# Window attention into a soft mixture of experts on one core: score maxima in nine 128-column products, and three smaller reorderings

## The chip, the core and the metric

The kernel runs on one core of a Trainium2 chip. The metric is the device time of one execution in microseconds (us). Five in-order engines work side by side: TensorE (PE), which multiplies; VectorE (DVE); ScalarE (ACT); GpSimd (POOL), which here also issues most DMAs; and SyncE (SP), which issues the first loads and the stores. They wait for each other through semaphores. TensorE writes to PSUM, eight banks of 2 KB per partition; ACT and DVE read it there.

## What is computed

Shapes: 8 batches, 8 heads, 576 positions, 64 dimensions a head; 4608 rows of 512, 8 experts with 4 slots each, hidden width 1024. Cut to the computation:

```
scores = q @ k.T / 8
mask   = (0 <= i - j < 64)
scores = where(mask, scores, -1e9);  scores -= max over keys
attn   = exp(scores) / (sum + 1e-9)
x      = attn @ v, heads side by side: (4608, 512)

logits = x @ phi                                  # (4608, 32)
d      = exp(logits - max over rows) / sum        # dispatch, per column
slots  = d.T @ x                                  # (32, 512)
out_e  = relu(slots_e @ w1_e) @ w2_e              # 8 experts
c      = exp(logits - max over slots) / sum       # combine, per row
out    = c @ slot_out                             # (4608, 512)
```

## The kernel before, in words

The work is ordered by hand: instructions stand on each engine in the order in which the Python code emits them. The main loop (lines 535 to 624) has 32 iterations `n`, one for each pair of heads (8 batches of 4 pairs), and is a software pipeline. Iteration `n`

- has POOL join pair `n + 1` into transposable order (`join`, L101) and issue coming loads (`load_qk`, `load_v`, `load_w`) and copies of v shifted by half a chunk (`shift_v`);
- turns k and then q of pair `n` through PE (`turn`, L259) into PSUM banks `kb` and `qb`, from which ACT copies them to `kT` (L269) and to `qz` (L266, two copies, one per head, with zeros between so that one product serves both heads);
- finds the largest score of each query of pair `n - 1`: `st_mask` (L274, L275) writes the mask into the PSUM tile `mx`, `st_max` (L291) adds the scores, and DVE reduces them into `m` (L296, `keep_max`);
- turns the maxima of pair `n - 2` through PE (`st_shift`, L300) into the tile `av`, and copies nine rows of them to `rt` (L303, `keep_shift`);
- computes the masked and shifted scores of pair `n - 3`: constants `lh` times `rt` (L320), plus keys times queries (L323), in `sc`, with the ninth chunk apart (`score_last`, L311 and L312), followed by two exponentials on ACT (L328, and L316 for the ninth chunk) into `pt`;
- multiplies `pt` of pair `n - 4` with v (`st_av`, L340) into `av`, and DVE divides by the sums (`st_norm`, L349 and L350) into `x_b`;
- turns `x_b` of pair `n - 5` (L363), and DVE copies it to `xt` (L370).

From `n = 8` on, each batch of rows also has four steps, `fi` = 0 to 3: the logits (L379; copied at L384; maximum at L388 and L389), the dispatch exponentials `dd` (L395) and the turned logits (L403, L408), the slot sums `si` (turned dispatch weights in the same bank as `qb`, copied by ACT to `dT`, L420; sums at L459; accumulation `acc`, L469), and the combine weights (L431, L438, L447). Turns, logits and sums share a ring of two PSUM banks, taken in turn: a product can start when the reader of the bank's last content is done.

A chunk is 64 queries of both heads; its windows lie in 128 keys. In the kernel before, the maxima are found per half chunk: 32 queries of two heads are 64 columns, and their keys lie in a window of 96. So there are 18 products of 64 by 96, ten groups of 96 in the two banks of `mx`, and one reduction over 960 elements; the mask comes from constants of its own (`sel`, `wm`, `wb`), built on POOL and DVE at the start.

After the loop the last pairs and the last two batches are finished, then the experts run: `first`, `turned` and `second` (L796 to L825). The second expert layer of the last `NH` experts, whose weights come last, is done by column halves (`half`, L844): slot outputs for 256 columns, then output rows for these columns (`cps`, L856: product, scaling on ACT or DVE, DMA from SP), then the other 256.

Of the kernel before, what the change touches and what calls it, by code (L numbers as in the profile page):

```python
# [20 lines left out]
def kernel(  # L21
# [114 lines left out]
    for t_, src in reversed(tuple(zip(firsts, (q, k)))):  # L136
# [9 lines left out]
    lh = const.tile([128, 9, 128], FP16, name="lh")  # L146
    nc.vector.memset(lh, 0.0)
    warm = lh[:, 0:4, :].rearrange("p i x -> p (i x)")
    NQ = 4
    qzs = [pqk.tile([128, 2 * S], FP16, name=f"qz{i}") for i in range(NQ)]  # L150
    kTs = [pqk.tile([128, 64 + S], FP16, name=f"kT{i}") for i in range(NQ)]
    sides[0] = (pil.tile([GP, RQ, 2, Dh], FP16, name="qi", tag="qi"),
                pil.tile([GP, RQ, 2, Dh], FP16, name="ki", tag="ki"))
    KR = 74
    nc.scalar.activation(lh[64:KR], ident_h[64:KR, 64:KR - 1].unsqueeze(2).broadcast_to([KR - 64, 9, 128]),
                         AF.Copy, scale=-1.0)
    nc.vector.memset(qzs[0], 0.0)
    nc.vector.memset(kTs[0][:, 0:64], 0.0)
    for t_, src, eng in zip(sides[0], firsts, (nc.scalar.copy, nc.vector.tensor_copy)):
        eng(out=t_, in_=src.rearrange("p (h r d) -> p r h d", h=2, r=RQ))  # L160

    ctr = pmo.tile([128, 2 * S], FP16, name="ctr")
    wb = ctr[0:32, 0:96]
    nc.gpsimd.memset(wb, 0.0)
    nc.gpsimd.affine_select(out=wb, in_=wb, compare_op=ALU.is_gt, fill=NEG,
                            base=0, pattern=[[1, 96]], channel_multiplier=-1)
    nc.gpsimd.affine_select(out=wb, in_=wb, compare_op=ALU.is_ge, fill=NEG,
                            base=64, pattern=[[-1, 96]], channel_multiplier=1)
    mb = ctr[0:64, 96:224]
# [6 lines left out]
    NR = 2  # L176
    sel = const.tile([128, 4, 32], FP16, name="sel")
    wm = const.tile([128, 5, 96], FP16, name="wm")
    for t in (0, 64):
        nc.vector.tensor_copy(out=sel[t:t + 32],  # L180
                              in_=ident_h[t:t + 32, t:t + 32].unsqueeze(1).broadcast_to([32, 4, 32]))
        nc.vector.tensor_copy(out=sel[t + 32:t + 64].rearrange("p (t l) x -> p t (l x)", t=2),
                              in_=ident_h[t + 32:t + 64, t + 32:t + 34].unsqueeze(2).broadcast_to([32, 2, 64]))
        nc.vector.memset(wm[t + 32:t + 64], 0.0)
        nc.vector.tensor_copy(out=wm[t:t + 32], in_=wb.unsqueeze(1).broadcast_to([32, 5, 96]))
    nc.vector.memset(wm[32:33, 0, 0:64], NEG)
    nc.vector.memset(wm[32:34, 0, 0:32], NEG)
    av = pav.tile([128, 2, 512], FP32, name="av", tag="av")
    mx = pmx.tile([128, 2, 512], FP32, name="mx", tag="mx")
    nc.vector.memset(mx[:, 1, 384:480], 0.0)  # L190
    ms = [const.tile([128, 33], FP16, name=f"m{i}") for i in range(2)]
    for t_ in ms:
        nc.vector.memset(t_[:, 10:33], 0.0)
    for t_, z_ in zip(kTs[1:], qzs[1:]):
        nc.vector.memset(t_[:, 0:64], 0.0)
        nc.vector.memset(z_, 0.0)
    nc.vector.memset(av[64:128, :, 260:325], 1.0)
    rts = [const.tile([128, 128], FP16, name=f"rt{i}") for i in range(NR)]
    for rt in rts:
        nc.vector.memset(rt, 0.0)  # L200
    for i in range(3):
        nc.vector.memset(vrs[i][:, :, 64], 1.0)
    for i in range(2):
        nc.vector.memset(vss[i][:, :, 64], 1.0)
        nc.vector.memset(vss[i][0:64, 0, 0:64], 0.0)
    lgs = pf.tile([128, 192], FP32, name="lgs")
    nc.vector.memset(lgs[0:96, 128:192], -3.0e38)
    dd = pf.tile([128, 256], FP16, name="dd")
    nc.vector.memset(dd[:, 192:256], 0.0)
    run = pmo.tile([128, 3], FP32, name="run")  # L210
    stat, nmax = run[:, 0:1], [run[:, 1:2], run[:, 2:3]]
    nc.vector.memset(nmax[1], 1.0e30)
    nc.vector.memset(stat, 0.0)
# [65 lines left out]
    def heads(p, o, w):  # L279
        a = qzs[p % NQ][:, 2 * o:2 * o + 2 * w]  # L280
        return a if w == 32 else a.rearrange("p (t l x) -> p l t x", t=2, l=2)

    def turned_max(p):
        return rts[p % NR][:, :].rearrange("p (t l x) -> p l t x", t=2, l=2)

# [622 lines left out]
```

## Time and profile before

| | |
|---|---|
| three timed runs | 194.35, 195.71, 192.37 us; median 194.35 |
| profiled execution, time | 192.44 us |
| profiled execution, span of the core | 190.7 us |
| busy: PE, PEld, DVE, ACT, POOL | 155.2, 116.2, 139.8, 129.3, 129.8 us |
| granted TensorE clock, mean | 0.889 |
| DMA | 41.14 MB, mean 216 GB/s |

The profile shows one execution. A row of the order of time gives start and length in us, engine, line, operation, result and operands with their shapes; in brackets stands the idle time of the engine just ahead of it and what ended it. Rows of equal instructions in a row are merged (x6). PEld is the loading of weights into TensorE. The ends of products are modelled and overlap, so starts are what to read on PE.

### The profile page before, as it was taken

The page shows a single profiled execution, that of the slowest core. Times are in us where ns is not written, and L with a number is a line of the kernel's source. Part 1 is how long each engine was busy: PE and PEld are TensorE (multiplying, and loading weights), DVE is VectorE, ACT ScalarE, POOL GpSimd, SP SyncE. Part 2 cuts the span into 40 slices and gives each one's busy share as a digit, 9 for nine tenths or more (in the row PEclk, how much of TensorE's full clock was granted, in tenths as well). Part 3 has the DMA queues.
Part 4 walks back from the last instruction along what each step waited for, and adds up shares of the span by engine and source line. Part 5 has one row for each costly group of instructions (what it writes and reads, how often), then busy time and mean ns, then how long its engine had stood idle before and what let it go on. Part 6 is the DMA issues. An engine that isn't in the chain of part 4 may idle for free.

```text
span 190.7 us, 6941 instructions
## 1 busy us (share of the span) xinstructions
PE 155.2 (81%) x2897; PEld 116.2 (61%) x2897; DVE 139.8 (73%) x322; ACT 129.3 (68%) x244; POOL 129.8 (68%) x254
## 2 busy tenths in 40 slices
PE   1858888988898898988989779997888999999400
PEld 0538777867687677776868657676666446564000
DVE  4786688888799979978879987887775754689500
ACT  5672787879778797887977888787664052668400
POOL 8989999976979879888897877965988440000000
PEclk9975699999999999999999999999999699555555
DMA  6999999999999999999999999999999999999996
GB/s 149 148 184 184 201 199 184 173 224 177 184 220 183 183 221 180 185 223 178 182 215 188 188 217 211 198 213 213 217 218 199 198 198 180 249 342 342 399 415 269
DMA packets 64447, 41.14 MB, mean 216 GB/s; under 512 B 38816, under 2 KB 61856, under 8 KB 62880
## 3 DMA queue, kind: packets, MB, share of 16 engines
q0 software_dynamic: 58320, 30.68, 118.1%
q1 hardware_dynamic: 6096, 10.03, 14.6%
q8 instruction: 22, 0.36, 0.7%
q14 instruction: 9, 0.07, 0.1%
HBM read 61.93 MB, written 9.44 MB: 374 GB/s over the span
## 4 chain that ended last, share of the span: by engine, by line
PE 38%; DVE 32%; ACT 11%; issue 10%; POOL 2%; DVEq 0%; ACTq 0%; POOLq 0%
DVE m L296 9%; DVE x_b L350 8%; PE cp L861 7%; PE av L340 6%; ACT qz L266 3%; PE sc L320 3%; PE hh L800 3%; PE sc L323 3%; DVE rt L303 2%; PE ops L823 2%; ACT pt L328 2%; DVE rc L349 2%; PE mx L291 2%; PE qb L259 2%; ACT pt L316 2%
## 5 line engine op out<-in xcount | busy, mean ns | idle before, releaser
L266 ACT ACTIVATE qz<-qb 64x576 f16<-64x576 f16 x64 | 41.2, 643 | 1.8 <-PE qb L259 1.2
L296 DVE TENSOR_REDUCE m<-mx 128x10 f16<-128x960 f32 x32 | 36.8, 1149 | 0.6 <-PE mx L291 0.6
L328 ACT ACTIVATE pt<-sc 128x1024 f16<-128x1024 f32 x29 | 29.6, 1022 | 9.4 <-PE sc L323 8.7
L269 ACT ACTIVATE kT<-kb 128x576 f16<-128x576 f16 x32 | 20.8, 650 | 13.6 <-PE kb L259 13.2
L350 DVE TENSOR_TENSOR x_b<-av,rc 128x640 f16<-128x640 f32 x31 | 25.6, 824 | 1.1
L259 PE MATMUL qb<-ident_h,qi 96*128 96x96 f16 x192 | 14.2, 212 | 8.9 <-DVE acc L469 3.5
L303 DVE CAST rt<-av 9x128 f16<-9x128 f32 x30 | 8.7, 289 | 16.5 <-PE av L300 15.7
L117 POOL DMA_DIRECT2D vr<-in_v_dram x16 | 20.0, 1249 | 0.0
L323 PE MATMUL sc<-qz,kT 128*128 128x128 f16 x232 | 18.6, 223 | 0.7 <-issue 0.7
L320 PE MATMUL sc<-rt,lh 128*128 128x128 f16 x232 | 18.6, 225 | 0.6 <-DVE rt L303 0.6
L291 PE MATMUL mx<-kT,qz 128*64 128x96 f16 x576 | 18.7, 211 | 0.0
L340 PEld LDWEIGHTS <-pt 128*64 128x64 f16 x576 | 12.7, 110 | 9.3 <-ACT pt L316 4.4
L259 PEld LDWEIGHTS <-qi 96*128 96x128 f16 x192 | 11.5, 101 | 10.6 <-issue 9.5
L323 PEld LDWEIGHTS <-kT 128*128 128x128 f16 x256 | 16.5, 100 | 0.9 <-issue 0.9
L108 POOL COPY qi<-qs 96x384 int32<-96x384 int32 x31 | 15.6, 503 | 1.8 <-DMA qs<-in_q_dram 0.9
L320 PEld LDWEIGHTS <-lh 128*128 128x128 f16 x256 | 16.2, 100 | 0.7 <-DVE lh L228 0.4
L108 POOL COPY ki<-ks 96x384 int32<-96x384 int32 x31 | 15.6, 503 | 1.1
L865 ACT ACTIVATE ob<-cp,rcs 128x256 f32<-128x256 f32 (+1 forms) x27 | 13.2, 546 | 3.9 <-PE cp L861 3.6
L291 PEld LDWEIGHTS <-qz 128*64 128x64 f16 x576 | 15.6, 113 | 0.5 <-issue 0.4
L259 PE MATMUL kb<-ident_h,ki 96*128 96x96 f16 x192 | 14.6, 216 | 1.1 <-DVE xt L370 0.6
L340 PE MATMUL av<-vr,pt 128*64 128x65 f16 x279 | 15.4, 197 | 0.0
L340 PE MATMUL av<-vs,pt 128*64 128x65 f16 x279 | 13.7, 198 | 1.8 <-ACT pt L316 1.8
(198 smaller groups left out, 367.8 us busy)
## 6 DMA issues: line engine op xcount, KB each, us to landing
w<-in_moe_w_dram POOLq DMA_DIRECT2D x12, 1024.0 KB, 15.2
vr<-in_v_dram POOLq DMA_DIRECT2D x16, 288.0 KB, 11.8
out_dram<-ob SPq DMA_DIRECT2D x6, 768.0 KB, 7.0
ks<-in_k_dram POOLq DMA_DIRECT2D x15, 288.0 KB, 9.5
qs<-in_q_dram POOLq DMA_DIRECT2D x15, 288.0 KB, 10.3
out_dram<-ob SPq DMA_DIRECT2D x11, 384.0 KB, 4.3
w<-in_moe_w_dram POOLq DMA_DIRECT2D x8, 512.0 KB, 13.8
xt<-in_k_dram SPq DMA_DIRECT2D x1, 288.0 KB, 3.1
```

The costliest lines, as they stand in the source:

```text
L108: nc.gpsimd.tensor_copy(out=d_, in_=s_.rearrange("p h r d -> p r h d"))
L117: nc.gpsimd.dma_start(out=vrs[b % 3][:, c0:c1, 0:64], in_=src[:, c0:c1, :])
L259: nc.tensor.transpose(tp[:, j, :], src[:, j].rearrange("p h d -> p (h d)"), ident_h[0:GP, 0:GP])
L266: nc.scalar.activation(dst[r, hl], src[r], AF.Copy, scale=scale)
L269: nc.scalar.activation(kTs[p % NQ][:, 64:64 + S].rearrange("p (g j) -> p g j", j=RQ), ps[:, 0:RQ * GP].rearrange("p (j g) -> p g j", j=RQ) ...
L291: nc.tensor.matmul(mx[64 * t:64 * t + 64, i // 5, 96 * (i % 5):96 * (i % 5) + 96], heads(p, o, 32), kT[:, o:o + 96], start=False, stop=Tru ...
L296: nc.vector.reduce_max(ms[p % 2][:, 0:10].rearrange("p (h c) -> p h c", h=2), mx[:, :, 0:480].rearrange("p h (c x) -> p h c x", x=96), axi ...
L320: nc.tensor.matmul(sc[:, i // 4 - o, 128 * (i % 4):128 * (i % 4) + 128], lh[:, i, :], turned_max(p), start=(i % 4 == 0), stop=False, skip_ ...
L323: nc.tensor.matmul(sc[:, i // 4 - o, 128 * (i % 4):128 * (i % 4) + 128], kTs[p % NQ][:, 64 * i:64 * i + 128], heads(p, 64 * i, 64), start= ...
L328: nc.scalar.activation(pts[p][:, 0:8, :, :], sc[:, :, :].rearrange("p u (c l x) -> p (u c) l x", l=2, x=64), AF.Exp)
L340: nc.tensor.matmul(av[r0:r0 + 64, hl, 65 * (i // 2):65 * (i // 2) + 65], pt[:, i, hl, :], values(b, h, i), start=True, stop=True, skip_gro ...
L350: nc.vector.tensor_tensor(out=x_b[:, :, 128 * hp:128 * hp + 128].rearrange("p c (l d) -> p l c d", l=2), in0=avv[:, :, :, 0:64], in1=rc[:, ...
```

## The change

1. *Maxima.* `st_max` takes eight products of 128 columns (64 queries of two heads) by 128 keys, and `st_max_last` the ninth, which stands in the free end of a bank of `av`, ahead of `st_av`. The mask comes from constants that the scores use too (`lh`, `rt`) and one small tile `low`; `st_mask` moves from ahead of `st_av` to just ahead of `st_max`, behind the shift. DVE reduces 1024 elements (`keep_max`) and, ahead of that, the ninth chunk's 128 (`keep_max_last`). `qz` is laid out by 64 queries and head. `lh` has nine constant rows instead of ten.
2. *The ninth chunk's scores* go to the end of the bank of `qb` instead of `av`, behind the turn of q. In the iterations with `fi` 0 and 2, ACT copies the shift to `rt` (before: DVE) and makes `qz` and the last exponential only behind it; the logits are copied by ACT instead of DVE.
3. *First constants and joins.* Fewer constants are made ahead of the loop; `vr`, `vs`, `av` and softmax constants follow in iterations 2 and 3. The joins of pairs 3 and 4 and some loads move to the ends of iterations 1 and 2.
4. *The end.* `NH` is 2 instead of 3; the last three output rows of the second quarter are made in whole width after both halves (15 rows by halves instead of 18).

The diff, cut to its core:

```diff
 def st_mask():
-    st = sel.rearrange("p a x -> p (a x)")
-    nc.tensor.matmul(mx[:, 0, 0:480], st[0:64], wm[0:64, 0:5, :], ...)
-    nc.tensor.matmul(mx[:, 1, 0:384]..., st[64:128], wm[64:128, 1:5, :]..., ...)
+    for r, u, keys in ((slice(0, 64), 0, lh[0:64, 0:4, :]),
+                       (slice(64, 128), 1, low[64:128, 1, :].unsqueeze(1).broadcast_to([64, 4, 128]))):
+        nc.tensor.matmul(mx[:, u, :]..., (low[r, 0, :] if u else rts[0][r, :]), keys, ...)
 def st_max(p):
-    for i in range(9):
-        for t in range(2):
-            o = 64 * i + 32 * t
-            nc.tensor.matmul(mx[64 * t:64 * t + 64, i // 5, 96 * (i % 5):96 * (i % 5) + 96],
-                             heads(p, o, 32), kT[:, o:o + 96], ...)
+    for i in range(8):
+        nc.tensor.matmul(mx[:, i // 4, 128 * (i % 4):128 * (i % 4) + 128], queries(p, i),
+                         kTs[p % NQ][:, 64 * i:64 * i + 128], ...)
+def st_max_last(p, to):
+    nc.tensor.matmul(to, rts[0][0:64, :], lh[0:64, 8, :], start=True, ...)
+    nc.tensor.matmul(to, queries(p, 8), kTs[p % NQ][:, 512:640], ...)
+def keep_max_last(p, to):
+    nc.vector.reduce_max(ms[p % 2][:, 8:9], to, axis=AXX)
...
-NH = 3
+NH = 2
...
-    if n + 1 < NP:
+    if n + 1 < NP and n not in (2, 3):
         join(n + 1)
...
         keep_main(n - 3, sc)
-        score_last(n - 3, av[:, 0, 328:456])
-        keep_last(n - 3, av[:, 0, 328:456])
...
     turn(sides[n][0], qb)
-    keep_q(n, qb)
-    if n >= 1:
-        st_mask()
+    if n >= 3:
+        score_last(n - 3, s8)
+    late = fi in (0, 2)
+    if not late:
+        keep_both()
+    m8 = av[:, 0, 328:456]
+    if n >= 1:
+        st_max_last(n - 1, m8)
     if n >= 4:
         st_av(n - 4, av)
...
         st_shift(n - 2, av[64:97, 1, 384:512])
-        keep_shift(n - 2, av[64:97, 1, 384:512])
+        keep_shift(n - 2, av[64:97, 1, 384:512], nc.scalar.copy if fi in (0, 2) else nc.vector.tensor_copy)
+    if late:
+        keep_both()
...
     if n >= 1:
+        keep_max_last(n - 1, m8)
+        st_mask()
         st_max(n - 1)
...
         keep_max(n - 1)
+    if n == 1:
+        join(3)
+        load_v(0, (1,))
+        load_qk(3)
+    elif n == 2:
+        constants(2)
+        join(4)
+        load_qk(4)
+        shift_v(0, 0)
+        load_w(1)
+    elif n == 3:
+        constants(3)
     if fi == 0:
-        keep_logits(lg, nc.vector.tensor_copy)
+        keep_logits(lg, nc.scalar.copy)
...
-        for j0, j1 in ((0, 1), (1, 3), (3, 6), (6, 9)) if h == g == 0 else thirds:
+        for j0, j1 in ((0, 1), (1, 3), (3, 6), (6, 9)) if h == g == 0 else thirds[0:3 - g]:
             cps(g, j0, j1, DH * h, DH * h + DH)
+cps(1, 6, 9)
```

`keep_both` is `keep_q(n, qb)` followed by `keep_last(n - 3, s8)`; `s8` is the last 128 fp32 columns of the bank of `qb`.

160 lines of the change are left out of this document (75 added, 85 removed).

## The prediction

> **What bounds the kernel now.** I read the page first, then busy times in stretches, then one batch of the loop on each engine in order of time, then the queues of the start.
>
> ```profile
> span 190.7 us, 6941 instructions
> ...
> GB/s 149 148 184 184 201 199 184 173 224 177 184 220 183 183 221 180 185 223 178 182 215 188 188 217 211 198 213 213 217 218 199 198 198 180 249 342 342 399 415 269
> ```
>
> ```profile
> 12.00:22.00 10.00, 8.20 (x94) 6.85 (x95) 6.77 (x21) 4.95 (x8) 9.85 (x16) 0.50 1.72 184
> ...
> 65.67:81.53 15.86, 14.48 (x327) 11.83 (x324) 13.65 (x29) 13.40 (x26) 13.76 (x27) 1.00 1.54 195
> ```
>
> The columns of the stretches are length, busy PE, PEld, DVE, ACT, POOL, granted clock, DMA share, GB/s. A batch of four loop iterations takes 15.86 us; no engine fills it, four are within 2.5 us of it. So the batch is set by hand-offs between in-order queues, and the change must be costed along those, not by busy time. I call the four iterations of a batch by what they add: logits, exp, slots, combine (n mod 4 = 0, 1, 2, 3, for n = 8 to 31: six batches). One batch on PE, from the start of its `kb` turn to that of the next batch:
>
> ```profile
> 83.71 0.43 PE L259 MATMUL kb<-ident_h,ki 96*128 96x96 f16 x6
> ...
> 85.35 0.42 PE L259 MATMUL qb<-ident_h,qi 96*128 96x96 f16 x6
> 86.03 0.36 PE L274 MATMUL mx<-wm,sel 64*128 64x480 f16 x1 [0.26 <-DVE m L296]
> ...
> 86.66 0.22 PE L300 MATMUL av<-ident_h,m 128*33 128x128 f16 x1
> ...
> 87.64 0.43 PE L259 MATMUL kb<-ident_h,ki 96*128 96x96 f16 x6
> ...
> 89.95 0.41 PE L259 MATMUL qb<-ident_h,qi 96*128 96x96 f16 x6 [0.59 <-DVE lgs L384]
> 90.30 0.37 PE L274 MATMUL mx<-wm,sel 64*128 64x480 f16 x1
> ...
> 90.89 0.22 PE L300 MATMUL av<-ident_h,m 128*33 128x128 f16 x1
> ...
> 91.42 0.43 PE L259 MATMUL kb<-ident_h,ki 96*128 96x96 f16 x6
> ...
> 94.31 0.22 PE L340 MATMUL av<-vs,pt 128*64 128x65 f16 x1 [0.21 <-ACT pt L316]
> ...
> 94.59 0.22 PE L300 MATMUL av<-ident_h,m 128*33 128x128 f16 x1
> ...
> 95.70 0.43 PE L259 MATMUL kb<-ident_h,ki 96*128 96x96 f16 x6
> ...
> 99.57 0.43 PE L259 MATMUL kb<-ident_h,ki 96*128 96x96 f16 x6
> ```
>
> The iterations take 3.93, 3.78, 4.28 and 3.87 us. PE stands three times: the mask for the maxima (L274) waits for the last reduction to free `mx`, `qb` waits for a bank that DVE still reads (logits, slots), and `av` waits for ACT's last exponential, which reads a bank of `av`. ScalarE and VectorE in the same batch:
>
> ```profile
> 88.11 0.65 ACT L269 ACTIVATE kT<-kb 128x576 f16<-128x576 f16 x1 [0.60 <-PE kb L259]
> 89.06 1.02 ACT L328 ACTIVATE pt<-sc 128x1024 f16<-128x1024 f32 x1 [0.30 <-PE sc L323]
> ...
> 90.58 0.45 ACT L395 ACTIVATE dd<-lgs,run 128x192 f16<-128x192 f32 x1 [0.32 <-DVE run L389]
> ...
> 91.22 1.28 ACT L266 ACTIVATE qz<-qb 64x576 f16<-64x576 f16 x2
> 92.52 0.65 ACT L269 ACTIVATE kT<-kb 128x576 f16<-128x576 f16 x1
> 93.07 1.02 ACT L328 ACTIVATE pt<-sc 128x1024 f16<-128x1024 f32 x1
> 93.97 0.28 ACT L316 ACTIVATE pt<-av 128x128 f16<-128x128 f32 x1
> 94.13 0.31 ACT L420 COPY dT<-qb 128x160 f16<-128x160 f16 x1
> 94.30 1.32 ACT L266 ACTIVATE qz<-qb 64x576 f16<-64x576 f16 x2
> ```
>
> ```profile
> 86.99 0.29 DVE L303 CAST rt<-av 9x128 f16<-9x128 f32 x1 [0.39 <-PE av L300]
> ...
> 87.57 0.82 DVE L350 TENSOR_TENSOR x_b<-av,rc 128x640 f16<-128x640 f32 x1
> 88.31 1.15 DVE L296 TENSOR_REDUCE m<-mx 128x10 f16<-128x960 f32 x1
> 89.38 0.52 DVE L384 COPY lgs<-lg 128x128 f32<-128x128 f32 x2
> 89.93 0.35 DVE L388 TENSOR_REDUCE nb<-lgs 128x1 f32<-128x192 f32 x1
> ...
> 97.31 0.74 DVE L469 SCALAR_TENSOR_TENSOR acc<-acc,al,si 128x512 f32<-128x512 f32 x1
> ```
>
> **The change, part by part.** *The products.* The mask grows from 480 + 256 columns to 512 + 512, and 18 products become 8 of 128 columns, plus two small ones for the ninth chunk. Eight such products have a row, and so has ScalarE's copy of the shift:
>
> ```profile
> 100.00 0.45 PE sc L320 x8
> ```
>
> ```profile
> L303 ACT CAST rt<-kb x2: 256/256/256, 134.7 to 137.3; 9x128 f16<-9x128 f32 x2
> ```
>
> 1024 columns take 0.45 us, so mask and maxima after the shift take 0.05 + 0.45 + 0.45 = 0.95 us, where 90.89 to 91.42 was 0.53 with the mask ahead of it; the ninth chunk is 0.11 us ahead of `av`. On PE it is some +0.25 us per iteration.
>
> *The reduction.* 1024 elements for 960: 64 more at 1.15 us / 960, +0.08 us. The ninth chunk is a reduction of its own, 128 elements: at most the 0.35 us of the 192-element L388, at least the 0.12 us that 128 elements take by L296's rate; I take 0.22. DVE gains 0.3 us per iteration, loses the `rt` copy (0.29) in logits and slots and the logits copies (0.52) to ACT: 13.65 + 4 × 0.3 − 0.58 − 0.52 = 13.75 us a batch, no more than before.
>
> *The order.* Shift no longer stands behind a mask that waits for the reduction, and the last exponential reads `qb`, not `av`, so both PE waits (0.26 and 0.21 us) go. What is late next: in logits and slots the two `qz` copies and the last exponential stand on ACT behind the `rt` copy, which waits for the shift; the next `kb` takes `qb`'s bank and so waits for all three. In exp, the two logits copies stand ahead of `kT` on ACT. In slots, the last score product shares `qb` with the dispatch turn and waits for ACT's copy `dT`. These are waits that the built program has. I add them up, t = 0 at `kb` of logits:
>
> - Logits: `kb` to `qb` 1.64 (83.71, 85.35) less 0.11 for the last score, now later; `qb` 0.35 (89.95, 90.30), last score 0.11, ninth chunk 0.11, `av` 0.28 (94.31, 94.59): the shift starts at 2.38. ACT sees it 0.33 later (86.66, 86.99), 2.71; the copy holds ACT 0.20 of its 0.256; `qz` pair 2.91 to 4.23; exponential at 4.15 for 0.27; next `kb` 4.47. Before 3.93: +0.54.
> - Exp: PE needs 2.38 + 0.95 and reaches the next `kb` at 7.80, unhindered. ACT: logits copies to 4.71, `kT` at 4.47 + 0.47 (87.64, 88.11) = 4.94, main exponential at 4.47 + 1.42 (87.64, 89.06) = 5.89, for 0.90 (93.07, 93.97); `dd` and its two followers 0.64 (90.58, 91.22), `qz` 1.30 (91.22, 92.52), last exponential 0.16 (93.97, 94.13): `kT` of slots at 8.89, 1.1 us after its `kb` instead of 0.47.
> - Slots: `kT` ends 9.54, exponential 9.44 to 10.34, `dT` to 10.65; the last score starts 10.70, shift 10.70 + 0.11 + 0.11 + 0.28 = 11.20, `rt` 11.53, `qz` 11.73 to 13.05, exponential to 13.24, next `kb` 13.29. From `kb` of logits to here it was 95.70 − 83.71 = 11.99: +1.30.
> - Combine: DVE's reciprocal waited in slots for the end of ACT's `rt` (11.79, and 0.05 to hand over, as from 89.38 + 0.52 to 89.95); then 0.29 (0.58 from 86.99 to 87.57, less the copy), 0.74 (87.57, 88.31), 0.22 and 1.15 (88.31, 89.38, + 0.08) put `acc` at 14.24; 0.74 and a hand-over later `qb` starts, 15.03 (PE is there at 14.82); + 0.85 to the shift, + 0.95: 16.83.
>
> 16.83 against 15.86: **+0.97 us a batch, six batches +5.8 us**. Bounds: with ACT's two logits copies at the price of `dT` (0.31 each), `rt` at 0.256 and the exponential unoverlapped it is +1.3 a batch; with the ninth reduction, copies and exponential at their least, and half of the `dT` wait hidden, +0.5. So +3 to +8.
>
> The Trainium skill's page "PSUM — Partial Sum Buffer", in its section on bank collisions, says that no two engines may work in one bank and quadrant at once, reads included. The trace agrees where it can (`av` stood 0.21 us for ACT's read of other columns). That is why the reciprocal waits for `rt`; without the rule it would start 0.3 us earlier, `acc` would be no obstacle, and the sum would be 0.2 us a batch less, 1.2 us in all.
>
> *The start.* DVE's first constants are fewer and end earlier, and pair 3 is joined ahead of two loads. But pair 2's q (11.58) waits for DMA either way, and pair 4's join now stands on POOL ahead of `load_qk(4)`, the first shift of v, a weight load, v and phi.
>
> ```profile
> L117 POOL DMA_DIRECT2D vr<-in_v_dram x16 | 20.0, 1249 | 0.0
> ```
>
> ```profile
> qs<-in_q_dram POOLq DMA_DIRECT2D x1, 288.0 KB, 9.2
> ```
>
> ```profile
> 9.46 0.67 POOL L96 DMA_DIRECT2D qs<-in_q_dram  x1
> ...
> 11.58 0.50 POOL L108 COPY qi<-qs 96x384 int32<-96x384 int32 x1 [0.93 <-DMA qs<-in_q_dram]
> ...
> 21.71 0.52 POOL L108 COPY ki<-ks 96x384 int32<-96x384 int32 x1
> ...
> 24.71 0.43 PE L259 MATMUL kb<-ident_h,ki 96*128 96x96 f16 x6
> ```
>
> The q rows of pair 4 land 9.2 us after their issue at 9.46; issued perhaps 0.6 us earlier, 18.1 to 18.7. Behind that join wait about 5.3 us of POOL work (two k and q issues at 0.67, v issue 1.25, and by like prices the v shift, a weight and phi) until pair 5 is joined at about 24.5 instead of 21.71; its `kb` ran at 24.71 and now needs the join's 0.5 us: 25.0. POOL, busy 9.85 of 10 us there, takes back what DVE gives. I count 0, as 25.0 stands to 24.71; bounds −1.5 (the join waits little) and +1.5 (the delay reaches pair 6).
>
> *Light iterations* (n = 4 to 7) lose the mask wait but stand behind POOL: 0. *After the loop* the ninth chunk of the last pair adds a product and a reduction, +0.3. *The end.* Eight 512-column products in place of eight 256-column ones ahead of the first output cost about 8 × 0.03 us there; the second half starts with eight products and three output rows less before it, and 0.79 MB leaves in whole rows (399 GB/s against 342: −0.3 us). I take −0.3, bounds −1.0 to +0.5. **Sum: +5.8 us.**
>
> The profiled execution took 192.44 us around its span of 190.7; the three runs have a median of 194.35, 1% more. With the profiled one the four average 193.7, and I set the sum on that: 199.5 us.
>
> **The rivals.**
> *ACT's waits are covered; the freed shift decides.* Then the fullest queue sets the batch: DVE 13.75, PE 14.48 + 4 × 0.25 = 15.5 at the modelled busy time, less what that counts double. At 14.7 it is −1.2 a batch, −7 us: 186.5. For it: both PE waits that it removes are in the rows. Against it: ACT had 0.30 to 0.60 us idle ahead of `kT` and `pt` only, and is given 0.2 + 0.4 us more and made to wait twice. It decides if `kb` of exp and combine starts as soon as PE is done with `lg` and `si`.
> *Half of the stalls and an early start.* +0.4 a batch (+2.4), start −1.5: 194.6, no change. For it: my chain adds starts and slots from other iterations, and one hidden hand-over in each of its four steps is worth the difference of 0.5 us a batch. The Trainium skill's "TensorE: Matmul & The Clock Gate" (part 1) has the clock rise to full after about 3.4 us of sustained work; here PE was busy 8.20 of 10 us from 12 to 22 at 0.50, so the trace does not agree closely. If a denser start freed the clock 3 us sooner, that would be up to 1.5 us of PE, the same gain as this rival's.
> *The start adds to the loop.* +1.5 us of POOL delay and +1.3 a batch: 193.7 + 9.3 = 203.
>
> **How the numbers follow.** The forecast with its bounds (+3 to +8, start −1.5 to +1.5, not all at one end), 196 to 203: 0.50. No change by the second rival: 0.27. Faster by the first: 0.13. Beyond 203: 0.10. Two per cent, about what a measurement of this kernel can tell from no change, is 3.9 us: within 189.8 to 197.6 lie the second rival and 0.03 of the forecast's chance. Faster 0.13, same 0.30, slower 0.57. The range leaves out the first rival and half of the worst: 191 to 204.
>
> **What would show it.** In a batch of the new trace: `kb` of exp and combine waiting for ACT's last exponential (about 0.6 us each), the last score of slots waiting for `dT`, `kb` to `kb` about 4.5, 3.3, 5.5, 3.5 us; no wait of the mask for L296's successor, none of `av` for ACT; on POOL the join of pair 4 waiting for DMA near 16 to 19 us. I am wrong if the exp and combine turns start without a wait, or a batch comes in under 15.9 us.

## The result, and the profile after

| | before | after |
|---|---|---|
| timed runs | 195.03 us (192.37 to 196.34, 6 runs) | 203.81 us (201.72 to 204.74, 6 runs) |
| ratio after / before | | 1.054, 95% interval 1.045 to 1.064 |
| profiled execution | 192.44 us, span 190.7 | 203.72 us, span 201.9 |

The kernel became slower by 5.4%; the forecast was 199.5 us, some 3% slower than its base of 193.7. The direction and the waits were forecast, the size was not. By the medians the change costs 8.8 us, by the two profiled executions 11.3 us. The starts of PE's rows say where the 11.3 us of span came from. The columns are the starts of `kb` of n = 8 and n = 31, of the first expert product (`hh`), of the first product of an output row (`cp`), and the end.

| us | n = 8 | n = 31 | hh | cp | end |
|---|---|---|---|---|---|
| before | 35.92 | 128.47 | 149.64 | 160.90 | 190.66 |
| after | 37.16 | 138.52 | 161.39 | 173.32 | 201.94 |
| added in the stretch | +1.24 | +8.81 | +1.70 | +0.67 | -1.14 |

In the loop no engine has become full. The span of after, and the stretch of one batch with the columns of the forecast (length, busy PE, PEld, DVE, ACT, POOL, granted clock, DMA share, GB/s):

```profile
span 201.9 us, 6389 instructions
```

```profile
71.85:89.21 17.36, 15.50 (x290) 12.48 (x288) 14.08 (x29) 14.32 (x30) 13.73 (x27) 1.00 1.39 179
```

PE has 1.0 us more of busy time than before, ACT 0.9, DVE 0.4; the batch has 1.5 more. One batch of after in the order of time on PE (columns as in the rows of before: start, length, engine, line, operation, result and operands, shapes, idle time ahead and what ended it):

```profile
76.54 0.42 PE L248 MATMUL kb<-ident_h,ki 96*128 96x96 f16 x6 [0.65 <-ACT pt L302]
...
79.96 0.42 PE L248 MATMUL kb<-ident_h,ki 96*128 96x96 f16 x6
...
81.77 0.42 PE L248 MATMUL qb<-ident_h,qi 96*128 96x96 f16 x6
82.76 0.22 PE L297 MATMUL qb<-rt,lh 128*128 128x128 f16 x1 [0.57 <-ACT dT L406]
...
85.75 0.41 PE L248 MATMUL kb<-ident_h,ki 96*128 96x96 f16 x6 [0.54 <-ACT pt L302]
...
89.23 0.42 PE L248 MATMUL kb<-ident_h,ki 96*128 96x96 f16 x6
...
90.66 0.42 PE L248 MATMUL qb<-ident_h,qi 96*128 96x96 f16 x6
90.92 0.22 PE L297 MATMUL qb<-rt,lh 128*128 128x128 f16 x1
90.98 0.22 PE L298 MATMUL qb<-qz,kT 128*128 128x128 f16 x1
91.12 0.23 PE L276 MATMUL av<-lh,rt 64*128 64x128 f16 x1
91.28 0.23 PE L277 MATMUL av<-kT,qz 128*128 128x128 f16 x1
91.44 0.22 PE L326 MATMUL av<-vs,pt 128*64 128x65 f16 x1
...
91.72 0.22 PE L286 MATMUL av<-ident_h,m 128*33 128x128 f16 x1
...
91.88 0.39 PE L264 MATMUL mx<-lh,rt 64*128 64x512 f16 x1
91.88 0.39 PE L264 MATMUL mx<-low 64*128 64x512 f16 x1
92.20 0.62 PE L272 MATMUL mx<-kT,qz 128*128 128x128 f16 x8
...
93.91 0.41 PE L248 MATMUL kb<-ident_h,ki 96*128 96x96 f16 x6 [0.65 <-ACT pt L302]
```

From `kb` to `kb`: exp 3.42, slots 5.79, combine 3.48, logits 4.68, together 17.37 us; before 3.78, 4.28, 3.87, 3.93, together 15.86. The two steps without a wait became shorter than before, the two that end with a wait for ACT's last exponential much longer. ScalarE and VectorE around the slot step show why:

```profile
82.40 0.31 ACT L406 COPY dT<-qb 128x160 f16<-128x160 f16 x1
83.83 0.26 ACT L289 CAST rt<-av 9x128 f16<-9x128 f32 x1 [1.12 <-PE av L286]
84.11 1.30 ACT L255 ACTIVATE qz<-qb 64x576 f16<-64x576 f16 x2
85.42 0.28 ACT L302 ACTIVATE pt<-qb 128x128 f16<-128x128 f32 x1
```

```profile
84.12 0.22 DVE L335 RECIPROCAL rc<-av 128x10 f32<-128x10 f32 x1 [1.06 <-ACT rt L289]
...
85.11 0.28 DVE L283 TENSOR_REDUCE m<-av 128x1 f16<-128x128 f32 x1
85.31 1.21 DVE L280 TENSOR_REDUCE m<-mx 128x8 f16<-128x1024 f32 x1
```

PE's last score waits for `dT`, ACT then stands idle 1.12 us for the shift that follows it, does `rt`, both `qz` copies and the exponential one after the other, and only then (85.70) is `qb`'s bank free for the next `kb` (85.75).

At the start POOL waits for pair 4's transfers, as forecast, and behind the loop one wait appears that the forecast did not have: in iteration 30 DVE waits 2.83 us for the factor of the old maxima (L600), which ACT now computes behind `qz` and the exponential. The rows of POOL and of DVE:

```profile
17.35 0.50 POOL L108 COPY ki<-ks 96x384 int32<-96x384 int32 x1 [1.88 <-DMA ks<-in_k_dram]
19.03 0.51 POOL L108 COPY qi<-qs 96x384 int32<-96x384 int32 x1 [1.18 <-DMA qs<-in_q_dram]
...
24.82 0.50 POOL L108 COPY ki<-ks 96x384 int32<-96x384 int32 x1
```

```profile
138.65 0.22 DVE L335 RECIPROCAL rc<-av 128x10 f32<-128x10 f32 x1 [2.83 <-ACT vr L600]
```

The profiled executions of e9 and e14 below ran some 2% longer than the same kernels' timed ones, so their ends are not compared with others.

### The profile page after: what moved, and what is told of

Its sections match the earlier page's. It is cut to its first block, busy times and chain, and to the rows that moved or that the text cites. A ratio compares the mean times of both kernels' runs of the same rounds, so it can differ in the third digit from the quotient of the medians.

```text
span 201.9 us, 6389 instructions
## 1 busy us (share of the span) xinstructions
PE 167.4 (83%) x2630; PEld 122.3 (61%) x2630; DVE 139.5 (69%) x317; ACT 136.4 (68%) x267; POOL 127.7 (63%) x250
## 4 chain that ended last, share of the span: by engine, by line
PE 50%; ACT 22%; DMA 7%; issue 6%; POOL 5%; DVE 4%; ACTq 0%; POOLq 0%
ACT qz L255 11%; DMA qs<-in_q_dram 7%; PE cp L877 6%; PE av L326 5%; PE sc L309 5%; PE sc L306 5%; PE kb L248 4%; PE hh L816 3%; PE mx L272 3%; ACT pt L314 3%; PE tx L349 2%; ACT pt L302 2%; PE qb L248 2%; PE ops L839 2%; PE av L277 2%
## 5 line engine op out<-in xcount | busy, mean ns | idle before, releaser
L280 DVE TENSOR_REDUCE m<-mx 128x8 f16<-128x1024 f32 x32 | 38.9, 1216 | 2.6 <-PE mx L272 2.6
L248 PEld LDWEIGHTS <-ki 96*128 96x128 f16 x192 | 11.2, 101 | 15.8 <-issue 8.5
L272 PE MATMUL mx<-kT,qz 128*128 128x128 f16 x256 | 20.7, 226 | 0.0
L272 PEld LDWEIGHTS <-qz 128*128 128x128 f16 x256 | 15.0, 100 | 7.7 <-issue 7.7
L309 PEld LDWEIGHTS <-kT 128*128 128x128 f16 x256 | 16.6, 101 | 0.0
L335 DVE RECIPROCAL rc<-av 128x10 f32<-128x10 f32 x31 | 6.8, 219 | 12.6 <-ACT rt L289 7.7
L433 POOL COPY ctr<-ct 32x64 int32<-32x64 int32 (+1 forms) x28 | 6.6, 237 | 13.7 <-DVE ct L424 12.8
```

The costliest lines, as they stand in the source:

```text
L248: nc.tensor.transpose(tp[:, j, :], src[:, j].rearrange("p h d -> p (h d)"), ident_h[0:GP, 0:GP])
L272: nc.tensor.matmul(mx[:, i // 4, 128 * (i % 4):128 * (i % 4) + 128], queries(p, i), kTs[p % NQ][:, 64 * i:64 * i + 128], start=False, stop ...
L280: nc.vector.reduce_max(ms[p % 2][:, 0:8], mx[:, :, :].rearrange("p u (c y) -> p (u c) y", y=128), axis=AXX)
L309: nc.tensor.matmul(sc[:, i // 4 - o, 128 * (i % 4):128 * (i % 4) + 128], kTs[p % NQ][:, 64 * i:64 * i + 128], queries(p, i), start=False, ...
```

## The experiments

The theory behind the first four: the loop's excess is made by the order on ACT and the hand-off of `dT`, the start's by the joins. The rivals: PE's new products, or DVE's longer reductions. The kernel before was timed again beside each group of runs, with medians from 193.3 to 195.6 us, so the times are to be compared by the ratios, and small differences by the stretches of the profile. Positions of all kernels, from the starts of PE's rows; the four steps (logits, exp, slots, combine) are means over n = 8 to 27. Their sum is a batch; before 3.93, 3.78, 4.47, 3.80 = 15.98.

| | time us, ratio to before [95%] | n = 8 | n = 31 | end | steps, batch |
|---|---|---|---|---|---|
| after | 203.81, 1.054 [1.045, 1.064] | 37.16 | 138.52 | 201.9 | 4.68 3.42 5.79 3.47 = 17.36 |
| e1 | 208.04, 1.074 [1.068, 1.080] | 36.83 | 143.53 | 206.7 | 3.97 3.68 6.07 4.77 = 18.49 |
| e2 | 201.70, 1.041 [1.033, 1.049] | 38.08 | 137.99 | 200.5 | 3.97 4.02 5.10 4.11 = 17.20 |
| e3 | 199.01, 1.027 [1.019, 1.035] | 37.31 | 134.26 | 197.8 | 4.69 3.43 5.06 3.47 = 16.64 |
| e4 | 200.95, 1.037 [1.033, 1.042] | 33.58 | 135.78 | 199.4 | 4.85 3.42 5.79 3.47 = 17.53 |
| e5 | 199.29, 1.032 [1.019, 1.045] | 36.86 | 134.73 | 197.9 | 4.52 3.22 5.79 3.26 = 16.78 |
| e6 (before, new order) | 200.12, 1.037 [1.023, 1.050] | 34.03 | 134.66 | 197.8 | 5.00 3.01 6.18 3.02 = 17.22 |
| e7 | 205.92, 1.067 [1.053, 1.080] | 38.16 | 139.57 | 204.5 | 4.69 3.43 5.79 3.47 = 17.37 |
| e8 (before, constants) | 193.09, 1.000 [0.994, 1.005] | 34.27 | 127.08 | 191.2 | 3.93 3.78 4.54 3.78 = 16.03 |
| e9 | 192.27, 0.999 [0.996, 1.003] | 34.89 | 129.26 | 194.6 | 4.12 3.78 4.26 4.16 = 16.33 |
| e10 (before, constants and end) | 192.41, 1.000 [0.995, 1.005] | 34.69 | 127.32 | 189.7 | 3.93 3.78 4.55 3.72 = 15.97 |
| e11 | 191.94, 0.997 [0.991, 1.002] | 33.79 | 127.67 | 190.8 | 4.61 3.22 5.06 3.26 = 16.14 |
| e12 | 200.58, 1.044 [1.034, 1.054] | 36.34 | 137.91 | 198.9 | 4.69 3.43 5.79 3.47 = 17.37 |
| e13 | 193.15, 1.001 [0.997, 1.006] | 34.81 | 129.22 | 191.0 | 4.69 3.22 5.05 3.26 = 16.22 |
| e14 | 193.74 to 197.91, two runs, no ratio | | | | |

**e1, without the late order on ACT.**

```diff
-        late = fi in (0, 2)
+        late = False
```

> The changed kernel with ScalarE's q copies and last exponential ahead of the shift copy again in all iterations; the shift copy stays on ScalarE in logits and slots. Theory (the order on ScalarE): the waits of kb for the last exponential (0.65 and 0.54 us) go, but the shift copy now comes some 1.2 us later and the reciprocal and the division with it: a batch of 16.7 to 17.2 us where the changed kernel has 17.37. Rival (the new products themselves are longer on TensorE and set the batch): unchanged, 17.3 to 17.4.

It became slower still (ratio 1.074 for 1.054, batch 18.49); the theory fell in this form, and so did the rival. With `qz` and the exponential first, the copy of the shift that stays on ACT comes behind them, and the logits copies behind that:

```profile
94.77 1.29 ACT L255 ACTIVATE qz<-qb 64x576 f16<-64x576 f16 x2
96.07 0.28 ACT L302 ACTIVATE pt<-qb 128x128 f16<-128x128 f32 x1
96.38 0.26 ACT L289 CAST rt<-av 9x128 f16<-9x128 f32 x1
96.66 0.48 ACT L370 COPY lgs<-lg 128x128 f32<-128x128 f32 x2
97.17 0.65 ACT L258 ACTIVATE kT<-kb 128x576 f16<-128x576 f16 x1
```

So the late order is a help once the copy is on ACT.

**e2, ACT relieved altogether.** As e1, and the shift's and the logits' copies on DVE:

```diff
+            keep_shift(n - 2, av[64:97, 1, 384:512])
...
+            keep_logits(lg, nc.vector.tensor_copy)
```

> The changed kernel with the whole of what ScalarE was given taken back: q copies and last exponential early, shift copy and logits copies on VectorE; the new maxima, the new place of the last scores, joins and end stay. Theory (ScalarE's order and load carry the loss in the loop): a batch of 15.9 to 16.3 us, the program near 195 us, some 8 below the changed one. Rival (the new products are the cost): a batch of at least 17.0 us, program over 201.

The logits step is back at 3.97 (before 3.93), but exp and combine are at 4.02 and 4.11, and the batch at 17.20, the time over 201: the rival's numbers came, the theory's did not. The rival's reason does not follow from it, for PE also waits again for DVE's reads of the shared bank (0.53 us for `acc`, 0.41 for `lgs`) and still 0.71 us for `dT`. The load on ACT alone is not the excess. Which of the new products costs what, this run does not say.

**e3, the dispatch copy behind the last score product.**

```diff
         turn(sides[n][0], qb)
-        if fi == 2:
-            keep_dispatch(fb, qb[:, 576:736])
         if n >= 3:
             score_last(n - 3, s8)
+        if fi == 2:
+            keep_dispatch(fb, qb[:, 576:736])
```

> The changed kernel with the copy of the turned dispatch weights placed behind the last score product instead of ahead of it, so that the product does not wait for that copy; nothing else. Theory (each hand-off is paid in full): the wait of 0.57 us in slots goes, slots 5.2 us instead of 5.79, a batch of 16.8, the program 3 us shorter. Rival (another wait ends at the same time): less than 1 us.

The slot step falls from 5.79 to 5.06, a little below the theory's 5.2, nothing else moves, the loop from n = 8 to 31 loses 4.4 us. The score product now follows the turn of q at once:

```profile
80.48 0.42 PE L248 MATMUL qb<-ident_h,qi 96*128 96x96 f16 x6
80.74 0.22 PE L297 MATMUL qb<-rt,lh 128*128 128x128 f16 x1
```

The idle time of 0.57 us in after's row is counted from the modelled end of the turn. By starts the score came 0.99 us behind the turn there (81.77, 82.76) and comes 0.26 behind it here. That is a delay of 0.73 us, and the step paid it in full, for ACT's copy and everything behind the shift hung on it.

**e4, joins and loads of the first iterations as before.**

```diff
-        if n + 1 < NP and n not in (2, 3):
+        if n + 1 < NP:
             join(n + 1)
...
-        if n == 1:
-            join(3)
-            load_v(0, (1,))
-            load_qk(3)
```

(and the same for iteration 2's join, loads and shift of v)

> The changed kernel with joins, loads and the first shift of v in the places that they had before; constants stay reordered. Theory (pair 4's join waits for its DMA and holds up GpSimd's queue): iteration 8 starts 1.0 to 2.5 us earlier than the 37.16 us of the changed kernel, the loop unchanged behind it. Rival (the reordered joins gain and something else lost the time): iteration 8 starts later than 37.5.

n = 8 starts at 33.58, 3.6 us earlier, more than the theory's 1.0 to 2.5. Versions with after's start spread over 36.34 to 38.16, so the size is good to about 1 us. The loop behind it did not stay as it was: it became 0.8 us longer (logits 4.85 for 4.68), and the time fell by 2.9 us. POOL no longer waits for pair 4's transfers with other loads behind it; pair 4's join stands at 18.67 and pair 5's at 21.55:

```profile
18.67 0.50 POOL L108 COPY ki<-ks 96x384 int32<-96x384 int32 x1
...
21.55 0.52 POOL L108 COPY ki<-ks 96x384 int32<-96x384 int32 x1
```

**e5, the ninth chunk's mask with 128 rows.** In after the gaps between starts on PE are 0.14 from the last score product to the mask product (L276), 0.16 to the next (L277), 0.16 to `av`, 0.16 from the shift to the masks; where two products of equal shape follow each other it is 0.06. Is it the change of shape?

```diff
-        nc.tensor.matmul(to, rts[0][0:64, :], lh[0:64, 8, :], start=True, ...)
+        nc.tensor.matmul(to, low[:, 0, :], low[:, 1, :], start=True, ...)
...
+    nc.vector.memset(low[0:64], 0.0)
```

> The kernel after, with one edit: the mask product of the ninth chunk takes weights and keys of 128 rows (the lower 64 rows of both set to fit, zeros in the keys) in place of 64; result and columns as they were. In the trace of after, the starts of PE's products go 0.15 us from the ninth chunk's last score product to this mask product, 0.16 from it to the 128-row product behind it, where two 128-row products in a row lie 0.055 apart. Theory: PE pays about 0.1 us at each change between 64 and 128 rows, and all four steps hang on PE's way to the shift. Then the shift comes 0.2 us earlier in each iteration, the steps are about 4.5, 3.2, 5.6, 3.3 us (after: 4.68, 3.42, 5.79, 3.48), a batch 16.6 instead of 17.37, and the time is about 199 us. Rival: the 0.1 us belongs to a new result tile or to something else than the rows, or another engine takes over at once: batch 17.2 or more, time 202.5 or more.

```profile
93.38 0.22 PE L298 MATMUL qb<-rt,lh 128*128 128x128 f16 x1
93.44 0.22 PE L299 MATMUL qb<-qz,kT 128*128 128x128 f16 x1
93.49 0.22 PE L277 MATMUL av<-low 128*128 128x128 f16 x1
93.55 0.22 PE L278 MATMUL av<-kT,qz 128*128 128x128 f16 x1
93.97 0.22 PE L287 MATMUL av<-ident_h,m 128*33 128x128 f16 x1
```

From the last score product to the shift are now 0.53 us instead of 0.74 (90.98, 91.72): each change between 64 and 128 rows had cost 0.1. The product's operands changed tiles too (`rt` and `lh` to `low`), which this run does not separate from the rows. Exp and combine became 0.20 and 0.21 shorter, logits 0.16, slots not at all. From `kb` of exp to `dT` on ACT it is 5.86 us in after (76.54, 82.40) and 5.85 here (74.91, 80.76): what exp gains, the last score of slots waits for again, and the shorter way to the shift then gives slots 0.2 back. The time is 199.29 as expected from the theory, the batch a little above it (16.78 for 16.6).

**e6, the new order in the kernel before** (the ninth scores in `qb`, shift and logits copied by ACT, `qz` late in two iterations; maxima, constants, joins and end as before). The core of the edit:

```diff
-            score_last(n - 3, av[:, 0, 328:456])
-            keep_last(n - 3, av[:, 0, 328:456])
...
+            score_last(n - 3, s8)
...
+            keep_shift(n - 2, av[64:97, 1, 384:512], nc.scalar.copy if late else nc.vector.tensor_copy)
+        if late:
+            keep_both()
```

> The kernel before, with part 2 of the change alone: the ninth chunk's scores in the bank of qb, ACT copying the shift first in two of four iterations and the logits, qz and the last exponential behind; maxima, constants, joins and end as before. Theory: the excess of the loop is made by this order (the wait of the score product for the dispatch copy, ACT's longer way from the shift to the next kb): steps of 4.5, 3.4, 5.6, 3.4 us, a batch of 16.7 to 17.2 instead of 15.86, time 198 to 201 us. Rival: the excess is made by the maxima's new form (more products and changes of row size on PE, a longer reduction), the order alone costs at most 0.3 us a batch: 16.2 or less, time 195.5 or less.

```profile
82.68 0.42 PE L259 MATMUL kb<-ident_h,ki 96*128 96x96 f16 x6 [1.04 <-ACT pt L316]
...
85.70 0.43 PE L259 MATMUL kb<-ident_h,ki 96*128 96x96 f16 x6
...
90.70 0.41 PE L259 MATMUL kb<-ident_h,ki 96*128 96x96 f16 x6 [1.14 <-ACT pt L316]
```

The order alone takes the batch to 17.22, 1.24 above before. The two steps without ACT's long way fall to 3.0 us, the other two rise to 5.0 and 6.2, further apart than the theory's steps; in the batch and the time it held. It also brings n = 8 forward by 1.9 us. The gain is there by `kb` of n = 5 (22.35 for 24.71); in before `av` stands 0.61 us for the last exponential shortly ahead of it (23.89), and here it does not. What made the rest was not traced. The new maxima add only 0.1 a batch to that: they slow exp and combine by 0.4 each, but in logits and slots this is cover under ACT's wait (1.04 and 1.14 us here, 0.54 to 0.65 in after).

**e7, the end as before** (`NH = 3`, 18 rows by halves).

> The kernel after, with part 4 undone: three experts and 18 rows by column halves, as before. From the first output row's product to the end the kernel before takes 29.8 us, after 28.6. The forecast had the new end worth 0.3 us (between a loss of 0.5 and a gain of 1.0). Theory: the new end is worth most of the 1.2 us: 29.5 to 29.9 us here, time 204.4 to 205. Rival: the later loop alone lets the last weights arrive in time, and the form of the end is worth nothing: 28.5 to 28.8 us, time within 0.3 us of after.

From the first output row to the end it takes 29.90 us, after 28.62, before 29.76: the new end is worth 1.2 to 1.3 us, the theory held for this stretch. The time moved by 2 us, beyond the theory's 205, since n = 8 came a microsecond later than in after, within that start's spread.

**e8, only the later constants in the kernel before.**

```diff
-    nc.vector.memset(av[64:128, :, 260:325], 1.0)
...
+        late_constants(n)
```

(the same memsets, and those of the softmax constants, at the ends of iterations 2 and 3)

> The kernel before, with one edit: the ones of v's tiles and of av, and the softmax constants, are set on DVE at the ends of iterations 2 and 3 in place of ahead of the loop; nothing else of the change. Theory: in the kernel before DVE's constants delay the first maxima, and the change's later constants are worth something that its joins lose again: the first reduction comes 0.7 to 1.5 us earlier, n = 8 starts at 34.5 to 35.3 us instead of 35.9, time 191.8 to 193. Rival: the joins and loads of POOL set the start once DVE is faster: n = 8 at 35.7 to 36.1, time as before.

n = 8 comes 1.65 us earlier, somewhat more than the theory's 0.6 to 1.4, and n = 31 still 1.4, but the time is that of before. The waits of PE (engine, line, what for, total us, times, longest) and the chain that ended last say where part of it went:

```profile
PE ops L828 <- DMA w<-in_moe_w_dram: 1.7, 1, 1.7
```

```profile
144.75 21.45 DMA w<-in_moe_w_dram
```

The last expert weights land at 166.2 us. In the kernel before they landed at 165.1, and the products that read them start at 165.11.

**e11, e5 + e3 + e4 together**, and **e12, the factor ahead of `qz` in iteration 30**:

```diff
-        if late:
+        if late and n != NP - 2:
             keep_both()
...
             nc.scalar.activation(fO, av[:, 1, 340:341], AF.Exp, bias=pO)
+            keep_both()
```

> The kernel after with three edits together, each of which ran alone: the dispatch copy behind the ninth chunk's score product, the ninth chunk's mask product with 128 rows, joins and loads of the first iterations as before. Alone they shortened the span by 4.1, 4.1 and 2.6 us. Theory: they are three separate costs and make up the whole excess over before: batch 15.8 to 16.1 us, n = 31 at about 127.5 to 129, span 190 to 192, time 191.5 to 193.5. Rival: what they take away is taken by something that comes late next (the last expert weights, which in the kernel before with later constants landed only at 166 us, or ACT in the iterations with its long way): span 194 or more, and PE waits for a weight transfer behind the loop.

e11 ends at 190.8 us, time 191.94, level with before: the three are separate costs and together as large as the excess of the time. They are not all that the change costs: e11's loop is still 1.3 us longer than before's (93.88 for 92.55) and its way from n = 31 to `cp` 2.2 us, which an n = 8 that is 2.1 us earlier and the shorter end make up for.

> The kernel after, with one edit: in iteration 30 ACT computes the factor of the old maxima (1 exponential of 128 by 1) ahead of qz and the last exponential, not behind them. In after, DVE's reciprocal waits 2.83 us for it in this iteration. Theory: this wait is a good part of the 1.7 us that after loses between the start of n = 31 and the first expert product: n = 31 starts 1.0 to 1.6 us earlier, time 202.2 to 202.8. Rival: DVE is not what the next steps wait for there: n = 31 and the end move by less than 0.5 us.

In e12 DVE's wait falls to 1.37 us:

```profile
136.42 0.22 DVE L335 RECIPROCAL rc<-av 128x10 f32<-128x10 f32 x1 [1.37 <-ACT vr L600]
```

n = 31 does not start earlier beyond its earlier n = 8, where the theory had put the gain; instead the way from n = 31 to the first expert product falls from 22.87 to 21.05 (before 21.17). So the place was not where the theory had it. The size is known only roughly. The way from `hh` to `cp` was 11.13 for 11.93 in addition, with a granted clock of 0.92 for 0.85 there; e1, e3, e4, e5 and e7 have 11.1 too, without this edit, but 23.5 to 23.9 ahead of `hh`. Over both stretches, n = 31 to `cp`, it is 34.80 in after, 34.57 to 35.06 in these five and 32.18 in e12. The same edit takes 34.59 in e11 to 32.99 in e13 below. So it is worth 1.6 to 2.6 us. The time, 200.58, fell by 3.2.

**e9, e11 with ACT relieved as in e2.**

> The kernel after with the three edits and ACT relieved as well: the shift and the logits copied by DVE, qz and the last exponential ahead of the shift in all iterations. The nine products, the longer reduction and the new end stay. Theory: ACT's order costs more than it gives, so without it the new maxima are worth something: batch 15.4 to 15.8 us, n = 31 at 125 to 127, time 188.5 to 191.5, the first version under before. Rival: qb then waits for DVE's copies of logits and sums again (0.5 us each in the run with ACT relieved), which gives back what ACT loses: batch 16.0 or more, time 193 or more.

The theory fell on the batch: 16.33, with PE waiting 0.39 us for `lgs` and 0.82 for `acc`, as the rival had it. The time, 192.27, lies between the two.

**e10, the kernel before with the later constants and the new end.**

> The kernel before with two parts: the later constants (which alone brought n = 8 1.65 us forward and then lost it, with PE waiting 1.7 us for the last weights) and the end of after (two experts and 15 rows by halves). Theory: with two experts split, the second halves come in less of a hurry and the end is 1.2 us shorter, so the earlier start is kept: 190.5 to 192 us, faster than before by 0.8 to 1.5%. Rival: the transfers are the bound, the last weights land at 165 us or later in whatever order, and the time stays within 0.5 us of before.

192.41 us, and PE still waited 1.4 us for weights: the theory fell. **e13, all four repairs (e11 + e12):**

> The kernel after with four edits together: dispatch copy behind the ninth chunk's score product, ninth mask product with 128 rows, joins and loads of the first iterations as before, and the factor of the old maxima ahead of qz in iteration 30. The first three together gave a span of 190.8 us; the fourth alone shortened the way from n = 31 to the first expert product by 1.8 us (22.87 to 21.05). Theory: the four are separate and nothing else is late: from n = 31 to the first expert product about 21 us, span 188.5 to 189.5, time 190 to 191, faster than before by 1 to 2%. Rival: the last expert weights are the floor (they landed at 164 to 166 us in the two versions of the kernel before with an earlier loop, and PE waited for them): the gain of 1.8 us turns into a wait of PE for a weight transfer, time 191.5 to 192.7, as in the three versions that ended there.

The stretch from n = 31 to `hh` is 20.89 for 22.61 in e11, so the gain of e12 is found again, and the time, 193.15, does not fall: the theory fell. The rival gave the right direction, and only part of the mechanism. n = 31 came 1.55 us later than in e11 (129.22 for 127.67, of which 1.0 at n = 8, in a start that is the same code), so most of the gain was gone before it could meet the weights, and PE's wait for them is 0.5 us, for one that lands at 165.7:

```profile
144.38 21.28 DMA w<-in_moe_w_dram
```

**e14, e13 with the last four weight transfers issued ahead of POOL's 9.5 us of other work.**

```diff
-    load_w(1)
+    load_w(5)
     oldr, lgM = old_rows()
-    load_w(2)
```

(and the `load_w(2)` that stood further down is taken out)

> The kernel of the four repairs with one more edit: POOL issues the last four weight transfers ahead of its work on the old slot sums (some 9.5 us of POOL behind the loop), not behind it; in the run of the four repairs they were issued at 141.7 to 144.4 us and landed 2.7 us apart, the last at 165.7. Theory: the transfers themselves are the floor (DMA share above 1 and 198 to 218 GB/s in every stretch up to then); issued 9 us earlier, the last one lands at 164 to 166 us all the same, and the time stays at 191.5 to 193.5. Rival: the late issue on POOL is the floor: the last one lands at 158 us or earlier, PE waits for no weight, and the time falls to 191 or less.

POOL's issues in e13, then in e14, and the transfer for which PE waited in e14:

```profile
141.69 3.56 POOL L69 DMA_DIRECT2D w<-in_moe_w_dram  x4
```

```profile
131.23 2.29 POOL L69 DMA_DIRECT2D w<-in_moe_w_dram  x3
134.96 0.87 POOL L69 DMA_DIRECT2D w<-in_moe_w_dram  x1 [1.44 <-DMA w<-in_moe_w_dram]
139.84 0.88 POOL L69 DMA_DIRECT2D w<-in_moe_w_dram  x1 [4.00 <-DVE mx L688]
```

```profile
132.64 32.79 DMA w<-in_moe_w_dram
```

The transfer for which PE waited was issued at 132.6 and landed at 165.4; in e13 the one of the same rank was issued at 142.6 and landed at 160.3. The last one was issued 4.5 us earlier than in e13 and landed at 170.7, 5 us later. Theory (164 to 166) and rival (158 or earlier) both missed this. Issued up to 10 us earlier, none landed earlier: a sign, from one execution of 197.91 us, that POOL's issue is not the floor. The old slot sums, now behind the loads, made PE wait 3.1 us more; the timed run took 193.74, where three runs of the kernel before beside it took 194.75 to 196.38. That the transfers' rate is the floor fits the issues and landings, though not the 5 us: in both kernels the last transfers, 512 KB each, land 2.5 to 2.9 us apart (some 195 GB/s, an estimate from this size and a gap of 2.7 us), and in e13 the DMA engines are full up to this point, at 198 GB/s, as in before in its stretch at 150 us:

```profile
148.00:158.00 10.00, 9.88 (x138) 4.17 (x135) 5.97 (x18) 3.23 (x7) 4.38 (x15) 0.83 1.26 198
```

It is not shown by an experiment with fewer bytes or larger packets; that was not tried. The page counts 38816 of 64447 packets under 512 bytes in before; the Trainium skill's page "DMA: Bandwidth & Descriptors", in "Why small descriptors are slow (HBM only)", puts a fixed cost on each packet, which no run here separates from the bytes.

## Why the forecast was too low

The sum said +5.8 us; it was +11.3 in the profiled executions: 3.0 more in the loop, 1.2 more at the start, 2.1 more behind the loop, 0.8 less at the end. By the medians of the timed runs it was +8.8.

- *The waits of the batch.* All as forecast: `kb` of exp and combine wait 0.65 and 0.54 us for ACT's last exponential (0.6 was said), the last score of slots 0.57 for `dT`, neither the mask nor `av` waits. The first rival, ACT's waits covered, was wrong at each of these places.
- *The products, the step that failed first: the price of the ninth chunk on PE.* The chain had "the ninth chunk is 0.11 us ahead of `av`" and, from the last score to the shift, 0.50 us (0.11 + 0.11 + 0.28). It took 0.80 (90.92 to 91.72). A 64-row product between 128-row ones costs 0.1 us at each of two changes, and the third 0.1 is a longer gap ahead of `av`, whose cause was not tried. I had priced columns and not shapes, though two rows of before held the sign: from `qb` to the 64-row mask it was 0.35 us (89.95, 90.30), where in after the same six products are followed by a 128-row one after 0.26 (90.66, 90.92). So the 0.35 in the chain of logits already held one such change, and PE was ahead by 0.1 us at `qb` as well; there the shift came only 0.11 us later than said (2.49 for 2.38). e5 took two of these changes away and got 3.5 us of the loop back. The forecast's "some +0.25 us per iteration" on PE was right for busy time (1.0 us a batch), but not for the way: exp and combine, which wait for no other engine once begun, grew by 0.41 and 0.45 us from e6 to after, and by 0.20 and 0.24 from e6 to e5. That mask and maxima behind the shift took 0.93 us for the 0.95 said (79.03, 79.96) was luck: the gap ahead of the masks was 0.16 for 0.05, and the masks, side by side, took 0.32 for 0.45.
- *ACT's way from the shift to the next `kb`*, too short by 0.1 us in slots (2.19 from 83.56 to 85.75, for 2.09): the copy held ACT 0.28 us, not 0.20, and the exponential began when the second `qz` copy had ended (84.11 + 1.30 = 85.41, 85.42), not 0.1 ahead, while ACT saw the shift after 0.27, not the 0.33 that was read from DVE's row. With the later shift, and a last score 0.1 us earlier than said, that makes slots 5.79 for 5.49; logits were 4.68 for 4.47, exp 3.42 for 3.33, combine 3.48 for 3.54. The loop came out at +8.8 for +5.8, beyond the upper bound of 8. The rule of the Trainium skill's page "PSUM — Partial Sum Buffer", in the section cited in the forecast, is what the program keeps to when DVE waits 1.06 us for `rt` in the bank of `av`; no run here shows what happens without the wait.
- *The start, counted 0, bounds -1.5 to +1.5.* It was +1.24, inside them by luck, as a difference of larger things: e8 and e6 gained 1.65 and 1.9 us by constants and order alone, e4 puts the joins at 3.6. The step that said pair 5's join at 24.5 and its `kb` at 25.0 came near (24.82 and 25.37, +0.66 for the +0.29 said). The other 0.6 us were added between n = 5 and n = 8 (11.79 for 11.21), where the light iterations had been counted 0.
- *After the loop, +0.3.* It was +2.4 from n = 31 to `cp`, and this is the second step that failed: the factor of the old maxima, behind `qz` on ACT, costs 1.6 to 2.6 of it (e12, and e13 against e11), and the forecast had no term for it. The line stood in the kernel; I had gone through what waits behind `qz` in the four steps, and not in the one iteration that has a further instruction there.
- *The end, -0.3.* It was -1.14, 1.2 to 1.3 by e7, beyond the bound of -1.0.
- *The rivals.* The third, 203 us, to which "beyond 203" gave 0.10, has the time, by 1.3 a batch and +1.5 at the start; the runs have 1.4 a batch and +1.2 at the start, so its mechanism is largely there, and +2.4 and -1.1 behind the loop, which it did not have. The second, no change, was wrong.

What was not considered at all is that the kernel before may stand at a floor. Five versions with different loops and starts (e8, e9, e10, e11, e13) have medians of 191.9 to 193.2 us, and in four of them PE waits 0.5 to 2.4 us for the last weights. If so, little of what the change might have won could have shown. The floor itself is not shown.

## What to carry to other kernels

Price a product by its neighbours: where the number of rows changes from one to the next, add the change (0.1 us here), and look for it in the gaps of starts of the old trace. When work moves to another in-order engine, list everything queued behind it in every iteration, the rare ones too, and go through to who frees the next bank. Before costing gains, find what lands last at the end of the kernel: in e8 a start that was 1.65 us earlier ended in a wait of 1.7 us for the last weights.

## What the runs showed of the hardware

- A product of 64 rows between products of 128 rows: 0.1 us lost at each change, 0.055 us from start to start without one (e5). Operands changed with the rows in e5; the gap of 0.35 for 0.26 behind `qb` in before, with other operands, speaks for the rows.
- The two masks of 64 rows each, in different halves of the array, start together (91.88 and 91.88), and the next product, of 128 rows, starts 0.32 us later (92.20). The Trainium skill's page "TensorE: Matmul & The Clock Gate" says in its part 3 that products in different row groups of the array run concurrently. The trace agrees by these starts.
- The gap of 0.15 from a product of 128 columns to `av`'s of 64 columns stayed in e5 (93.55 to the `av` group 0.15 later); whether it has the same cause was not tried.
- The idle time ahead of a PE row is counted from a modelled end: it says 0.57 us where the starts say 0.73, and removing the wait gave back 0.73 us per batch (e3).
- An edit that made PE's way 0.2 us shorter in each step gave 0.2 us for exp and slots together, since `dT` on ACT stood between them at the same distance (5.86 and 5.85 us, e5).
- Transfers issued up to 10 us earlier landed no earlier (132.64 + 32.79 us in e14, one execution).
